# Blank products ahead of the first loads, word conversions behind the masks, and mixing steps in another order in an attention and mixer kernel

## The chip, the cores and the metric

The kernel runs on one core of one Trainium2 chip. Times are device microseconds (us) of one execution. The kernel before the change took 691.07 us, the median of three runs (690.26 to 691.5). The profiled execution spans 688.8 us from its first to its last instruction; that span is what the profile's views divide up.

A core has five engines that run at the same time and wait for one another by semaphores: TensorE (PE in the profile; PEld is its loading of weights), VectorE (DVE), ScalarE (ACT), GpSimd (POOL) and SyncE (SP). Each takes the instructions of its own queue in the order in which the program has them. In this kernel SyncE, and ScalarE at the very start, also issue the transfers from and to the chip's main memory.

## The reference, cut to what matters

A linear attention with decay, in blocks, is followed by a low-rank mixing over the sequence and a two-layer channel network with a residual:

```python
# q, k, v: (4, 8, 768, 64) float32; lam: (8,)
for b in range(nb):                                   # blocks of the sequence
    intra = einsum('bhic,bhjc->bhij', qb, kb) * Dmask     # Dmask = lam ** (i - j), lower triangle
    intra = einsum('bhij,bhjd->bhid', intra, vb)
    inter = einsum('bhid,bhde->bhie', qb * lam_pow, kv_state)
    out[:, :, sl] = intra + inter
    kv_state = lam_block * kv_state + einsum('bhsd,bhse->bhde', kb * rev_pow, vb)

x  = out as (4, 768, 512)
h  = x.transpose(0, 2, 1) @ U @ V                     # U: (768, 32), V: (32, 768)
u  = x + h.transpose(0, 2, 1)
ch = maximum(u @ w_ch1, 0) @ w_ch2                    # (512, 2048) and (2048, 512)
result = u + ch
```

U, V, w_ch1 and w_ch2 are float64 in memory. The kernel reads them as pairs of 32-bit words and puts together float32 values from them ("words" below).

## The kernel before

The attention part works on 24 tiles of 128 positions, six for each of the four batch rows, all eight heads at once. For a tile s: `prep` transposes q and k on TensorE and copies them out on ScalarE (tiles "qt", "kt"); `scores` multiplies them ("pss"); `masked` multiplies by the decay mask on VectorE ("sm"); `intra` multiplies by v ("px") and `state` updates the running state ("pkv", "kv"); `inter` adds the part of the state, with q scaled on GpSimd ("qs").

After the last tile of a row, `low` multiplies the row by U ("pp"), `low_sum` adds up the parts ("pr") and splits the result in a high and a low half ("vp"); `mix` multiplies by V and adds to the tile ("pu"); `turn` transposes the mixed tile for the channel network ("put"). `aside` does one portion of the conversion of words.

The order in which the pieces stand in every queue:

```python
    pieces = [("prep", 0), ("scale", 0), ("scores", 0), ("inter", 0), ("masked", 0)]
    for s in range(NS):
        b, c = divmod(s, NT)
        done = s - NT - 1
        more = s + 1 < NS
        step = [("prep", s + 1), ("scale", s + 1)] * more
        step += [("mix", done)] * (done >= 0)
        step += [("low", b - 1)] * (c == 0 and b > 0)
        step += [("intra", s), ("state", s)]
        step += [("turned", done - 1)] * (done > 0)
        step += [("scores", s + 1)] * more
        step += [("aside", s)]
        step += [("inter", s + 1), ("masked", s + 1), ("fade", s + 1)] * more
        step += [("low_sum", b - 1)] * (c == 0 and b > 0)
        step += [("turn", done)] * (done >= 0 and done // TG < FG)
        pieces += step
    pieces += [("mix", NS - NT - 1)]
```

One step of the word conversion, with two passes on VectorE and two on ScalarE; the portions that follow it are VectorE's alone:

```python
        def one():
            hi = st["w"][:, :, 1]
            ...
            nc.vector.tensor_scalar(sc, hi, 20, 0x7FF, ALU.logical_shift_right, ALU.bitwise_and)
            nc.vector.tensor_scalar(m, hi, 0xFFFFF, 0x100000, ALU.bitwise_and, ALU.bitwise_or)
            ...
            nc.scalar.activation(out=sc_f, in_=sc, func=AF.Relu, bias=low_end, scale=-1.0)
            nc.scalar.activation(
                out=sc, in_=sc_f, func=AF.Relu, bias=high_end, scale=-float(1 << 23)
            )
```

V's last portions split the values in a high part (copied on ScalarE) and a low part (subtracted on VectorE), each for several groups of rows of "vp". The tiles in which each portion stands:

```python
        (u_side, (0, 2, 2, 2, 2)),
        (v_steps(), (1, 2, 3, 3, 4, 4, 4, 5, 6, 6)),
```

The start. lam becomes a row on all partitions by a product ("pl", "lamb"); `constants` and `powers` make the mask and the powers from it on VectorE with twelve scans:

```python
    nc.scalar.dma_start(out=lam_row[:, 0:H], in_=lam.unsqueeze(0))
    nc.vector.memset(lam_row[:, H:], 1.0)
    for name, engine in (
        ("q", nc.sync), ("k", nc.scalar), ("q", nc.sync), ("k", nc.scalar), ("v", nc.sync)
    ):
        load_next(name, engine)
    for name in "kvqkv":
        load_next(name)
    make_identity(nc, ident)
    make_gather()
    pl = one_bank([P, H], "pl", "pq")
    nc.tensor.matmul(out=pl, lhsT=lam_row[:, H:], rhs=lam_row[:, 0:H], start=True, stop=True)
    nc.vector.tensor_copy(out=lamb, in_=pl)
    constants()
    scale_k(0)
    powers()
```

The channel network begins while the last row is still being mixed. Each unit is 16 products "pz" and 8 products "pd", evacuated to "r" by ScalarE and VectorE; the pieces of the last row are put between them (unit, product, piece, tile):

```python
    rest = [
        (0, 4, "enter", None),
        (0, 4, "turn", c0 - 2), (0, 9, "low", b), (0, 14, "low_sum", b),
        (0, 18, "turn", c0 - 1), (0, 22, "mix", c0),
    ]
    at = [(1, 5), (1, 13), (1, 21), (2, 5), (2, 13), (2, 21)]
    for n, (unit, i) in enumerate(at):
        if n + 1 < NT:
            rest.append((unit, i - 3, "mix", c0 + n + 1))
        rest.append((unit, i, "turn", c0 + n))
    ...
    side = list(zip((0, 1, 2, 2, 3, 3, 4, 4), w1_steps(2)))
```

The rest of the kernel, the two layers of the network, is the same before and after.

Of the kernel before, what the change touches and what calls it, by code (L numbers as in the profile page):

```python
# [8 lines left out]
FP32 = mybir.dt.float32  # L9
# [5 lines left out]
P = 128  # L15
# [3 lines left out]
def kernel(  # L19
# [59 lines left out]
    def set_ends(t):  # L79
        nc.vector.memset(t[:, 0:1], 1151.0)  # L80
        nc.vector.memset(t[:, 1:2], 255.0 * (1 << 23))
        ends.append(t)
# [184 lines left out]
    set_ends(vp[:, S + C : S + C + 2].bitcast(FP32))  # L267
# [55 lines left out]

    def prep(s):
        qt, kt = (att.tile([P, HP, P], FP32, tag=n, bufs=2, name=n) for n in ("qt", "kt"))
        n = HP // parts(s)
        for a0 in range(0, HP, n):
            for name, dst, tag in (("q", qt, "pt" if a0 else "pq"), ("k", kt, "pu" if a0 else "pk")):
                pt = one_bank([P, n, P], "p" + name, tag)
                for a in range(a0, a0 + n):  # L330
                    nc.tensor.transpose(  # L331
                        out=pt[:, a - a0, :], in_=raw[s, name][:, 2 * a : 2 * a + 2, :],
                        identity=ident,
                    )
                nc.scalar.copy(dst[:, a0 : a0 + n, :], pt)  # L335
        st[s].update(qt=qt, kt=kt)
        for name in "qk":
            load_next(name)
# [95 lines left out]
    def low(b):  # L434

        pp = one_bank([P, C], "pp", "pq") if b < B - 1 else bank([P, C], "pp", "b2")
        for c in range(G):
            nc.tensor.matmul(
                out=pp[c * R : (c + 1) * R, :], lhsT=u_w[:, c, :], rhs=xs[b * NT + c],
                start=True, stop=False,  # L440
            )

        n = C // 2
        assert 2 * (NT - G) == G
        for i in range(G):
            c, cols = G + i // 2, slice(i % 2 * n, (i % 2 + 1) * n)
            nc.tensor.matmul(
                out=pp[i * R : (i + 1) * R, cols], lhsT=u_w[:, c, :],
                rhs=xs[b * NT + c][:, cols], start=False, stop=True,
            )  # L450
        pts[b] = tmp("pt")
        nc.scalar.copy(pts[b], pp)

    def low_sum(b):
        pr = one_bank([P, C], "pr", "pu") if b < B - 1 else bank([P, C], "pr", "b2")
# [11 lines left out]
    def mix(s):  # L467
        b, c = divmod(s, NT)
        pu = one_bank([P, C], "pu", "pu") if s < NS - NT else bank([P, C], "pu", "b2")
# [48 lines left out]
    for s in range(NS):  # L518
# [3 lines left out]
        step = [("prep", s + 1), ("scale", s + 1)] * more  # L522
        step += [("mix", done)] * (done >= 0)
        step += [("low", b - 1)] * (c == 0 and b > 0)
# [3 lines left out]
        step += [("aside", s)]  # L528
        step += [("inter", s + 1), ("masked", s + 1), ("fade", s + 1)] * more
        step += [("low_sum", b - 1)] * (c == 0 and b > 0)  # L530
        step += [("turn", done)] * (done >= 0 and done // TG < FG)
        pieces += step
    pieces += [("mix", NS - NT - 1)]
# [55 lines left out]
    for steps, at in (  # L589
        (u_side, (0, 2, 2, 2, 2)),  # L590
        (v_steps(), (1, 2, 3, 3, 4, 4, 4, 5, 6, 6)),
# [13 lines left out]
    lam_row = consts.tile([1, H + P], FP32, name="lam_row")  # L605
    nc.scalar.dma_start(out=lam_row[:, 0:H], in_=lam.unsqueeze(0))
    nc.vector.memset(lam_row[:, H:], 1.0)
    for name, engine in (
        ("q", nc.sync), ("k", nc.scalar), ("q", nc.sync), ("k", nc.scalar), ("v", nc.sync)
    ):  # L610
        load_next(name, engine)
    for name in "kvqkv":
        load_next(name)
    make_identity(nc, ident)
    make_gather()
    pl = one_bank([P, H], "pl", "pq")
# [95 lines left out]
    def run_units(units, side, every=lambda i: None):  # L712
# [10 lines left out]
        (0, 4, "turn", c0 - 2), (0, 9, "low", b), (0, 14, "low_sum", b),  # L723
# [3 lines left out]
    at = [(1, 5), (1, 13), (1, 21), (2, 5), (2, 13), (2, 21)]  # L727
# [6 lines left out]
    side = list(zip((0, 1, 2, 2, 3, 3, 4, 4), w1_steps(2)))  # L734
# [162 lines left out]
```

## Time and profile before

| What | Before |
|---|---|
| median of three runs | 691.07 us |
| profiled span | 688.8 us |
| TensorE busy, share of the span | 98% |
| VectorE busy | 73% |
| ScalarE busy | 42% |
| GpSimd busy | 16% |
| transfers | 131.24 MB, 191 GB/s on the mean |

In the views that follow, the first number of a line of a timeline is the start in us from the beginning of the span, the second the duration; then come the engine, the line of the program, the operation, what it writes and reads, and how many instructions are merged. A bracket gives the time for which the engine was idle before it and what ended that. In the chain of work that ended last, each line is a start, a duration and what the end of the program waited for at that time. In a table by windows, each engine has its busy time and its count of instructions.

Attention and the last mixing fill the first 162 us of the span. The channel network fills the rest.

### The profile page before, as it was taken

To read this page: it belongs to the slowest core of one execution; us is meant where nothing else is said; L and a number is where in the kernel's file an instruction comes from. 1 tells how busy PE (TensorE), PEld (TensorE's weight loads), DVE (VectorE), ACT (ScalarE), POOL (GpSimd) and SP (SyncE) were. 2 spreads that over 40 slices of the span, in tenths; PEclk is the share of its full clock that TensorE was granted. 3 is DMA by queue.
4 is the path that set the end of the run, shared out by engine and by line. 5 is a ranking of instruction groups with operands and counts; after the bars stand their busy time and mean duration, and the time that the engine had idled before them with its cause. 6 is when DMAs were issued, how large, how long until landed. Compare 5 with 4: busy or idle time off the path is not lost.

```text
span 688.8 us, 12548 instructions
## 1 busy us (share of the span) xinstructions
PE 673.1 (98%) x4802; PEld 544.4 (79%) x4802; DVE 502.4 (73%) x857; ACT 290.5 (42%) x543; POOL 112.0 (16%) x90
## 2 busy tenths in 40 slices
PE   8889999999999999999999999999999999999997
PEld 6768787877888888888888888888888888888885
DVE  6468898877999777777789354787586686775864
ACT  4557676655566444444456231232232322322320
POOL 4326565532000000000000000030030120300300
PEclk9999999999999999999999999999999999999999
DMA  9968876235577655555566999955254363453431
GB/s 215 215 163 209 213 199 168 88 119 194 202 256 259 214 199 199 207 206 207 204 234 240 319 310 354 339 172 187 101 178 132 91 205 101 143 166 97 161 90 62
DMA packets 131629, 131.24 MB, mean 191 GB/s; under 512 B 81330, under 2 KB 89522, under 8 KB 131570
## 3 DMA queue, kind: packets, MB, share of 16 engines
q1 hardware_dynamic: 129472, 129.92, 59.1%
q8 instruction: 38, 0.62, 0.4%
q10 hardware_dynamic: 2098, 0.52, 0.3%
q14 instruction: 21, 0.17, 0.1%
HBM read 80.09 MB, written 50.33 MB: 189 GB/s over the span
## 4 chain that ended last, share of the span: by engine, by line
PE 93%; DVE 4%; DMA 1%; ACT 1%; issue 1%; POOL 0%; ACTq 0%; SPq 0%; DVEq 0%
PE pz L667 26%; PE pz L800 13%; PE pz L798 13%; PE pd L802 13%; PE pd L677 13%; PE px L424 3%; PE pss L371 3%; PE pkv L389 1%; PE px L412 1%; PE put L487 1%; PE pq L331 1%; PE pk L331 1%; DVE sm L380 1%; PE pu L470 1%; DMA words<-in_moe_V_dram 1%
## 5 line engine op out<-in xcount | busy, mean ns | idle before, releaser
L667 PE MATMUL pz<-u_hl,w 128*128 128x512 f32 x768 | 190.8, 398 | 0.8 <-ACT r L673 0.8
L667 PEld LDWEIGHTS pz<-u_hl,w 128*128 128x128 f32 x768 | 144.1, 188 | 37.0 <-ACT r L673 1.8
L800 PE MATMUL pz<-w_hl,m 128*128 128x512 f32 x384 | 151.6, 396 | 0.0
L798 PE MATMUL pz<-w_hl,m 128*128 128x512 f32 x384 | 151.6, 396 | 0.0
L802 PE MATMUL pd<-w_d,m 128*128 128x512 f32 x384 | 150.0, 396 | 0.0
L781 ACT ACTIVATE m<-mt 128x512 fp32r<-128x512 f32 x96 | 60.7, 632 | 195.3 <-PE pd L802 144.9
L782 DVE SCALAR_TENSOR_TENSOR m<-rm,m 128x512 fp32r<-128x512 f32 x96 | 71.5, 745 | 54.2 <-ACT m L781 54.1
L822 POOL TENSOR_TENSOR o<-o,u 128x512 f32<-128x512 f32 x20 | 29.9, 1524 | 450.7 <-DVE o L820 450.7
L682 DVE SCALAR_TENSOR_TENSOR r<-pd,r 128x512 f32<-128x512 f32 x96 | 61.8, 685 | 56.5 <-ACT r L673 44.2
L677 PE MATMUL pd<-u_d,w 128*128 128x512 f32 x384 | 98.8, 397 | 0.0
L798 PEld LDWEIGHTS pz<-w_hl,m 128*128 128x128 f32 x384 | 72.3, 188 | 17.6
L800 PEld LDWEIGHTS pz<-w_hl,m 128*128 128x128 f32 x384 | 72.3, 188 | 17.6
L802 PEld LDWEIGHTS pd<-w_d,m 128*128 128x128 f32 x384 | 72.3, 188 | 17.6
L677 PEld LDWEIGHTS pd<-u_d,w 128*128 128x128 f32 x384 | 72.1, 188 | 17.3
L673 ACT ACTIVATE r<-pz 128x512 f32<-128x512 f32 x96 | 51.9, 593 | 74.0 <-PE pz L667 73.9
L783 DVE SCALAR_TENSOR_TENSOR m<-m 128x512 fp32r<-128x512 f32 x96 | 69.1, 720 | 0.9
L780 DVE TENSOR_SCALAR mt<-rm 128x512 uint32<-128x512 uint32 x96 | 46.1, 481 | 24.6 <-DMA rm<-r_d 24.4
L380 DVE TENSOR_TENSOR sm<-pss,mask 128x512 f32<-128x512 f32 x48 | 30.7, 679 | 4.3 <-PE pss L371 4.3
L424 PEld LDWEIGHTS px<-vraw,sm 128*64 128x64 f32 x768 | 25.6, 142 | 10.3 <-DVE sm L380 5.3
L424 PE MATMUL px<-vraw,sm 128*64 128x64 f32 x768 | 29.5, 230 | 3.6 <-DVE sm L380 3.6
L355 POOL TENSOR_TENSOR qs<-qt,powq 128x512 f32<-128x512 f32 x20 | 25.6, 1278 | 40.7 <-ACT qt L335 37.4
L192 ACT CAST w<-wt 128x512 fp32r<-128x512 f32 x32 | 19.9, 622 | 29.0 <-DVE wt L189 20.7
(84 smaller groups left out, 706.4 us busy)
## 6 DMA issues: line engine op xcount, KB each, us to landing
r_d<-r SPq DMA_DIRECT2D x96, 256.0 KB, 2.2
rm<-r_d SPq DMA_DIRECT2D x96, 256.0 KB, 2.7
words<-in_moe_w_ch_dram SPq DMA_DIRECT2D x30, 512.0 KB, 4.1
w_d<-w SPq DMA_DIRECT2D x16, 768.0 KB, 3.3
w_hl<-w_d SPq DMA_DIRECT2D x16, 512.0 KB, 6.7
vraw<-in_v_dram SPq DMA_DIRECT2D x24, 256.0 KB, 3.8
u_d<-x_nat SPq DMA_DIRECT2D x24, 256.0 KB, 3.4
u<-u_d SPq DMA_DIRECT2D x24, 256.0 KB, 4.1
```

Source lines behind the costliest of these rows:

```text
L424: nc.tensor.matmul(out=px[half[t], x, a, :], lhsT=sm[:, x, a, half[t]], rhs=vr[:, 2 * a + x, :], start=(first and a == 0), stop=(a == HP - 1),
L667: nc.tensor.matmul(out=acc[g][0], lhsT=w[:, n, ct, :], rhs=uhl[g][:, n, ct, :], start=(ct == 0 and n == 0), stop=(ct == CT - 1 and n == 1),)
L673: nc.scalar.mul(rs[g], acc[g][0], 1.0 + E)
L677: nc.tensor.matmul(out=acc[g][1], lhsT=w[:, 2, ct, :], rhs=ud[g][:, ct, :], start=(ct == 0), stop=(ct == CT - 1),)
L682: nc.vector.scalar_tensor_tensor(rs[g], acc[g][1], 4096.0, rs[g], ALU.mult, ALU.add)
L780: nc.vector.tensor_scalar(t.bitcast(U32), r.bitcast(U32), HI, None, ALU.bitwise_and)
L781: nc.scalar.activation(out=m[:, 0], in_=t, func=AF.Relu)
L782: nc.vector.scalar_tensor_tensor(m[:, 1], r, 0.0, hi, ALU.max, ALU.subtract)
L783: nc.vector.scalar_tensor_tensor(m[:, 2], hi, E, low, ALU.mult, ALU.subtract)
L798: nc.tensor.matmul(out=pz, lhsT=m[:, 0, cols], rhs=hl[:, 0], start=first, stop=False)
L800: nc.tensor.matmul(out=pz, lhsT=m[:, 1, cols], rhs=hl[:, 1], start=False, stop=end)
L802: nc.tensor.matmul(out=pd, lhsT=m[:, 2, cols], rhs=dd, start=first, stop=end)
```

## The change

It has four parts.

1. Blank products: a tile of zeros is multiplied by itself, four times before lam's product and once before each of the first four groups of transposes. They compute nothing that is used; they are there to have TensorE at work while the first loads are under way. The first loads are issued in another order: q and k of tile 0 first, then lam, and all later loads from SyncE.
2. The word conversion of U and V stands behind the masks of the next tile instead of ahead of them, and some portions stand one tile later, so that a mask does not wait for words on their way.
3. At the boundary of two rows, `low` comes first in the step and `low_sum` before `intra`, so that copies and splits lie beside other products. They take other banks of the accumulator memory.
4. The mix of tile 17 moves from the end of the attention part into the first unit of the channel network, and the mixes and turns of the last row spread over three more units instead of two. Portions of the third weight tile's words move to later units.

```diff
+    def keep_busy(n, tag="pss"):
+        out = (one_bank([P, C], "idle", tag) if tag == "pq" else two_banks("idle", tag)[:, 0])[:, 0:P]
+        for i in range(n):
+            nc.tensor.matmul(out=out, lhsT=blank, rhs=blank, start=True, stop=True)
 ...
+                if s == 0:
+                    keep_busy(1)
 ...
-        pp = one_bank([P, C], "pp", "pq") if b < B - 1 else bank([P, C], "pp", "b2")
+        pp = one_bank([P, C], "pp", "pu") if b < B - 1 else bank([P, C], "pp", "b2")
 ...
-        pr = one_bank([P, C], "pr", "pu") if b < B - 1 else bank([P, C], "pr", "b2")
+        pr = one_bank([P, C], "pr", "pt") if b < B - 1 else bank([P, C], "pr", "b2")
 ...
-        step = [("prep", s + 1), ("scale", s + 1)] * more
-        step += [("mix", done)] * (done >= 0)
-        step += [("low", b - 1)] * (c == 0 and b > 0)
+        step = [("low", b - 1)] * (c == 0 and b > 0)
+        step += [("prep", s + 1), ("scale", s + 1)] * more
+        step += [("mix", done)] * (0 <= done < NS - NT - 1)
+        step += [("low_sum", b - 1)] * (c == 0 and b > 0)
         step += [("intra", s), ("state", s)]
         step += [("turned", done - 1)] * (done > 0)
         step += [("scores", s + 1)] * more
-        step += [("aside", s)]
+        step += [("aside", s)] * (done >= 0)
         step += [("inter", s + 1), ("masked", s + 1), ("fade", s + 1)] * more
-        step += [("low_sum", b - 1)] * (c == 0 and b > 0)
+        step += [("aside", s)] * (done < 0)
         step += [("turn", done)] * (done >= 0 and done // TG < FG)
         pieces += step
-    pieces += [("mix", NS - NT - 1)]
 ...
-        (u_side, (0, 2, 2, 2, 2)),
-        (v_steps(), (1, 2, 3, 3, 4, 4, 4, 5, 6, 6)),
+        (u_side, (0, 2, 2, 3, 3)),
+        (v_steps(), (1, 2, 4, 4, 5, 5, 5, 6, 6, 6)),
 ...
+    blank = x_pool.tile([P, C], FP32, tag="x", name="blank")[:, 0:P]
+    nc.vector.memset(blank, 0.0)
+    nc.vector.memset(lam_row[:, H:], 1.0)
+    set_ends(vp[:, S + C : S + C + 2].bitcast(FP32))
+    load_next("q", nc.sync)
+    load_next("k", nc.scalar)
     nc.scalar.dma_start(out=lam_row[:, 0:H], in_=lam.unsqueeze(0))
-    nc.vector.memset(lam_row[:, H:], 1.0)
-    for name, engine in (
-        ("q", nc.sync), ("k", nc.scalar), ("q", nc.sync), ("k", nc.scalar), ("v", nc.sync)
-    ):
-        load_next(name, engine)
-    for name in "kvqkv":
+    for name in "qkvkvqkv":
         load_next(name)
     make_identity(nc, ident)
     make_gather()
-    pl = one_bank([P, H], "pl", "pq")
+    keep_busy(4, "pq")
+    pl = one_bank([P, H], "pl", "pk")
 ...
-        (0, 4, "turn", c0 - 2), (0, 9, "low", b), (0, 14, "low_sum", b),
+        (0, 4, "turn", c0 - 2), (0, 6, "mix", c0 - 1), (0, 9, "low", b), (0, 14, "low_sum", b),
 ...
-    at = [(1, 5), (1, 13), (1, 21), (2, 5), (2, 13), (2, 21)]
+    at = [(1, 5), (1, 16), (2, 3), (2, 14), (3, 3), (3, 10)]
 ...
-    side = list(zip((0, 1, 2, 2, 3, 3, 4, 4), w1_steps(2)))
+    side = list(zip((0, 3, 3, 3, 4, 4, 4, 4), w1_steps(2)))
```

More of the change, by code (lines that the diff above doesn't have):

```diff
@@ L266 @@
     v_hl, p_hl = vp[:, 0:S], vp[:, S : S + C]
-    set_ends(vp[:, S + C : S + C + 2].bitcast(FP32))
     ident = keep.tile([P, P], FP32, name="ident")
@@ L468, in mix @@
         b, c = divmod(s, NT)
-        pu = one_bank([P, C], "pu", "pu") if s < NS - NT else bank([P, C], "pu", "b2")
+        pu = one_bank([P, C], "pu", "pu") if s < NS - NT - 1 else bank([P, C], "pu", "b2")
         nc.tensor.matmul(
```

## The prediction

> **What bounds the kernel now.** I read the page first: the span, the busy time of each engine and the shares of the chain that ended last.
>
> ```profile
> span 688.8 us, 12548 instructions
> ...
> PE 673.1 (98%) x4802; PEld 544.4 (79%) x4802; DVE 502.4 (73%) x857; ACT 290.5 (42%) x543; POOL 112.0 (16%) x90
> ...
> PE 93%; DVE 4%; DMA 1%; ACT 1%; issue 1%; POOL 0%; ACTq 0%; SPq 0%; DVEq 0%
> ```
>
> TensorE is busy for 673.1 of 688.8 us. From 162 us on its only hole is the end of the last product, which the change does not touch, so all that can be gained lies in the other 15.7 us of idle time and in the time in which TensorE ran at a lower speed. I then read the timeline of the first 12 us (start, duration, engine, line, idle time before and what ended it).
>
> ```profile
> 0.73 0.53 ACTq L606 DMA_DIRECT2D lam_row<-in_lam_dram  x1
> ...
> 2.05 0.56 PE L617 MATMUL pl<-lam_row 1*128 1x8 f32 x2 [2.05 <-DMA lam_row<-in_lam_dram]
> ...
> 2.85 2.63 DVE L288 TENSOR_TENSOR_SCAN mask<-lamb,ident 128x128 f32<-128x128 f32 x8
> ...
> 5.46 0.69 PE L331 MATMUL pk<-ident,kraw 128*128 128x128 f32 x2
> ...
> 6.08 2.08 PE L371 MATMUL pss<-qt,kt 64*128 64x128 f32 x16
> ...
> 6.89 2.19 DVE L301 TENSOR_TENSOR_SCAN powq<-small 128x128 f32<-128x128 f32 x4
> ...
> 9.00 1.26 DVE L380 TENSOR_TENSOR sm<-pss,mask 128x512 f32<-128x512 f32 x2
> 9.00 1.06 PE L331 MATMUL pk<-ident,kraw 128*128 128x128 f32 x4
> ...
> 9.99 1.48 PE L424 MATMUL px<-vraw,sm 128*64 128x64 f32 x32
> ```
>
> Two things are to be seen. The eight score products took 2.08 us here and take 1.16 us in every later tile: TensorE starts at about half speed, and still has it in the transposes at 9.00 (1.06 us, later 0.60), no longer in the state products at 11.30 (0.63, as later). And two chains reach the first "px" together: the loads of k (last half used at 5.46, then scores, then the next transposes) and the chain from lam, which lands at 2.05 and goes through the mask scans (2.63), the power scans (2.19) and "sm" (1.26), ending at 10.26. Neither has slack: "px" starts at 9.99.
>
> Then the chain that ended last, in order of time, for the attention part:
>
> ```profile
> 24.06 4.58 DMA words<-in_moe_V_dram
> ...
> 29.38 0.55 DVE m L158
> 29.93 1.21 DVE sm L380 x2
> ...
> 31.18 1.76 PE px L424 x28
> ...
> 49.26 0.47 PE pu L470
> ```
>
> Tile 3 and 4 of the first batch row wait on words of U and V, which stand on VectorE's queue ahead of "sm"; "px" of tile 4, which would have followed the transposes at 29.1, starts at 30.59 and goes on only at 31.18. The end shows the first mixing product waiting for the low half of p (1.31 us of idle time in the timeline). Two windows of 3.41 us at the place where the granted clock steps down (busy time of PE, PEld, DVE, ACT, POOL, then the granted clock and DMA) show the second price of that wait:
>
> ```profile
> 27.69:31.10 3.41, 1.74 (x40) 1.29 (x30) 2.34 (x5) 1.96 (x6) 0.00 (x0) 1.00 1.07 248
> 31.10:34.51 3.41, 3.33 (x50) 3.21 (x52) 0.62 (x3) 1.76 (x4) 2.63 (x3) 0.50 0.78 183
> ```
>
> TensorE was busy in only 1.74 of 3.41 us, and the following 3.41 us ran at a granted clock of 0.50. Last, the timeline of TensorE alone after 75 us; the brackets are all its waits that the change aims at:
>
> ```profile
> 113.73 0.47 PE L470 MATMUL pu<-vp 128*128 128x512 f32 x1 [0.35 <-DVE vp L463]
> ...
> 135.22 0.50 PE L470 MATMUL pu<-vp 128*128 128x512 f32 x1 [0.87 <-DVE x_nat L473]
> ...
> 156.70 0.63 PE L487 MATMUL put<-ident,x_nat 128*128 128x128 f32 x4 [0.25 <-DVE x_nat L473]
> ...
> 161.11 1.23 PE L667 MATMUL pz<-u_hl,w 128*128 128x512 f32 x3 [0.77 <-ACT r L673]
> ```
>
> [...]
>
> **The change part by part.**
>
> *Start.* Four blank products stand before lam's product, four more before the transposes of tile 0. A 512-column pass of "pr" follows its neighbour after 0.47 us, so 128 columns are 0.118 us, a blank product with two passes 0.24 us at full speed and about 0.47 at half: an estimate from that row. They start at about 1.1 us (after one more memset) and keep TensorE busy to 1.1 + 4 x 0.47 = 3.0. But lam's load moves from the first to the third place on ScalarE's queue, behind both halves of k. Issues there take 0.42 to 0.53 us, so it is issued at 0.73 + 0.53 + 0.43 + gaps = 1.75 instead of 0.73: one us later at the least. If it also stands in the rings behind k's 256 KB, it lands with them: q and k of tile 0 are 512 KB, first packets came 1.1 us after the issue (1.85), at some 220 GB/s they are in at 4.2, and 0.35 us passes to the product: lam at about 4.5 instead of 2.05, 2.4 us later. Everything on the lam chain keeps its length (2.05 to 10.26, 8.2 us), so "sm" ends near 12.7 instead of 10.26. TensorE itself: lam's product to 5.1, four pairs of a blank (0.47) and two transposes (0.55) to 9.2, scores to 10.2 at full or 11.2 at half speed, next transposes 1 to 2 us: 11.3 to 13. So the first "px" is ready about 2.4 us later, whatever the clock is. With the lesser delay of lam it is 0.9. The full clock comes too late to matter. I take +2.3 us.
>
> *U's and V's words behind the masks.* At full speed a tile takes 4.29 us (18.96 to 23.25), the first tile after the boundary about 5.6. From "px" of tile 2 at 18.96, with no wait at all, "px" of tile 3 would be at 23.25, of tile 4 at 27.54, of tile 5 at 31.83, of tile 6 at 36.53 (no state product, 1.5 us of "pp"), of tile 7 at 42.16. It was at 49.73: 7.6 us lost. In the new order I walk the queues again. VectorE does sm, then the words, so "px" waits no more; but ScalarE has two passes over the words (0.46 each for U, 0.62 for V) that stand ahead of the copies of the next q and k (pitch 0.47, 1.05 together).
> - U: sm(3) ends 22.93, first word step 0.3, ScalarE's two to 24.2, copies to 25.25; scores of tile 4 were due at 24.82: 0.5 lost.
> - V: sm(5) ends 1.32 after its scores, words 0.35, ScalarE's two to 2.96, copies to 4.0; the next scores are due at 2.73: 1.3 lost.
> - Boundary: V's last steps follow sm(6) (to 1.3) and end at 2.55, ScalarE's two casts of 0.5 each to 3.6, "pt" to 4.2. Its sum product is due at 2.5, as low and low_sum now come before the first "px" of the new row: 1.7 lost.
> - V's low rows (four of 0.55) come after sm(7) and end at 3.6 after its scores, while the first mix is due at 1.65: 1.95 lost.
> That is 5.4 instead of 7.6: 2.2 gained. Two of the new waits are as long as the one that halved the clock; one more window at half costs what it cost before, 1.76 + 1.07 + 1.52 against 1.15 + 0.64 + 1.16, 1.4 us; I put half of that in: gain 1.5.
>
> *Boundaries 2 and 3.* low starts one us earlier, with the transposes between it and low_sum, so the copy "pt" (0.58) is covered, and the low half of p (two of 0.7) is finished long before the next mix. That takes away 0.35 twice, and about 0.1 twice of the wait for "pp": gain 0.9.
>
> *Last mixing.* mix of tile 17 leaves its place ahead of the first big product (wait 0.87) for a place inside it, and the turns spread over a fourth unit, which relieves VectorE, ScalarE and GpSimd where the 0.25 and the 0.77 arose. Turn 23 is issued with 14 products of 0.234 us to go, 3.3 us before its data is first needed; its low part takes 0.05 + 0.7 + 0.6 + 0.6 + 1.3, about 3.3: just in time. Gain 1.9, at the most.
>
> Sum: +2.3 - 1.5 - 0.9 - 1.9 = -2.0, 691.1 to **689.1 us**.
>
> **Rivals.** (1) lam is hardly late. For it: 32 bytes in one packet. Then the start costs 0.9 or, if the clock comes early enough to speed tile 0, nothing: 687.7 to 686.8. (2) The first row gains more: if GpSimd's passes no longer collide, the word steps are shorter (V's third took 1.33 us beside two GpSimd passes, against 0.36 for U's) and one of the four new waits falls away: about 687.5. Against it: they are ScalarE's, not VectorE's. (3) The new waits halve the clock twice and lam's chain lets it idle once more: 691 to 692. (4) VectorE becomes the bound after the front: it was busy 19.51 of 20 us from 180 to 200, and three word steps of the third weight tile and a turn and a half are pushed towards it. Late evacuations would cost one to two us; against it, no idle time of TensorE there in the trace and two sets of banks.
>
> **Range and chances.** Start 0.5 to 3, words gain 0 to 3.5, boundaries and last mixing gain 2 to 2.8: 684.8 to 692.1 with all ends at once, which is unlikely. I take 686.2 to 691.6. Two per cent is 13.8 us, nearly all the idle time there is; so within 2% has 0.98, the others 0.01 each.
>
> **What would show it.** In the timeline of the changed kernel: lam's product starting at 4 us or later, with TensorE idle between the blanks and it, and "sm" of tile 0 ending after 12 (step 1); score products at about 1.1 us only from tile 1 on; no wait of "px" for "sm" in tiles 3 to 5, but waits of "pss" for the copies of k, of "pr" for "pt", and of the first "pu" for "vp" (step 2); no such wait at the second and third boundary (step 3); no gap before the first big product (step 4). I am wrong if "px" of tile 0 starts near 10 us or earlier, or if a window at half clock stands in the first 60 us more than once.

## The result, and the profile after

The changed kernel took 690.25 us (median of four runs, 689.71 to 690.47) against 690.88 us (four runs, 690.26 to 691.5) for the kernel before, measured beside it. The ratio is 0.999 with a 95% interval of 0.9972 to 1.0007: no difference that these runs could show. The prediction was 689.1, and its range of 686.2 to 691.6 holds the result. The range also holds the time of the kernel before, though, and the gain of 2.0 us that the prediction's sum came to lies just outside the interval, which runs from 1.9 us less to 0.5 us more. The parts of the sum say more than the total.

The profile's page of the changed kernel says the same, the span, the busy times and the shares of the chain that ended last:

```profile
span 688.6 us, 12580 instructions
...
PE 674.0 (98%) x4818; PEld 546.5 (79%) x4818; DVE 498.8 (72%) x858; ACT 291.2 (42%) x543; POOL 112.2 (16%) x90
...
PE 94%; DVE 3%; ACT 2%; issue 1%; DMA 0%; ACTq 0%; DVEq 0%
```

The span is 0.2 us shorter, TensorE is busy for 0.9 us more, with the blank products counted in, and the chain is TensorE's as before. So gains and losses of the four parts cancelled. To see which gained, I read the start of four landmark instructions of TensorE in both timelines; the difference grows or shrinks between two landmarks by what lies between them.

| Landmark | Before | After | Difference | Share of the stretch |
|---|---|---|---|---|
| first state product "pkv" of tile 0 | 11.30 | 13.60 | +2.30 | start: +2.30 |
| "px" of tile 7 | 49.66 | 52.71 | +3.05 | words, first boundary: +0.75 |
| "px" of tile 23 | 133.20 | 135.18 | +1.98 | boundaries 2 and 3: -1.07 |
| "pd" of the fourth unit | 165.22 | 165.19 | -0.03 | last mixing: -2.01 |

The four lines in TensorE's timeline before:

```profile
11.30 0.63 PE L389 MATMUL pkv<-vraw,ks 128*64 128x64 f32 x16
...
49.66 1.15 PE L424 MATMUL px<-vraw,sm 128*64 128x64 f32 x32
...
133.20 1.15 PE L424 MATMUL px<-vraw,sm 128*64 128x64 f32 x32
...
165.22 2.04 PE L677 MATMUL pd<-u_d,w 128*128 128x512 f32 x8
```

and after:

```profile
13.60 0.64 PE L396 MATMUL pkv<-vraw,ks 128*64 128x64 f32 x16
...
52.71 1.15 PE L431 MATMUL px<-vraw,sm 128*64 128x64 f32 x32
...
135.18 1.15 PE L431 MATMUL px<-vraw,sm 128*64 128x64 f32 x32
...
165.19 2.04 PE L686 MATMUL pd<-u_d,w 128*128 128x512 f32 x8
```

The start, from the timeline of the changed kernel (start, duration, engine, line, operation, in brackets the idle time before it and what ended it):

```profile
0.74 1.09 ACTq L255 DMA_DIRECT2D kraw<-in_k_dram  x2
...
1.05 2.08 PE L327 MATMUL idle<-blank 128*128 128x128 f32 x8 [1.05 <-DVE blank L614]
...
1.85 0.61 ACTq L619 DMA_DIRECT2D lam_row<-in_lam_dram  x1
...
4.65 0.56 PE L626 MATMUL pl<-lam_row 1*128 1x8 f32 x2 [1.52 <-DMA lam_row<-in_lam_dram]
...
5.45 2.63 DVE L287 TENSOR_TENSOR_SCAN mask<-lamb,ident 128x128 f32<-128x128 f32 x8
...
8.58 2.93 DVE L300 TENSOR_TENSOR_SCAN powq<-small 128x128 f32<-128x128 f32 x4
...
8.85 1.58 PE L378 MATMUL pss<-qt,kt 64*128 64x128 f32 x16
...
11.43 1.26 DVE L387 TENSOR_TENSOR sm<-pss,mask 128x512 f32<-128x512 f32 x2
...
12.14 0.34 PE L431 MATMUL px<-vraw,sm 128*64 128x64 f32 x4 [0.67 <-DVE sm L387]
```

lam's load is issued at 1.85 and no longer at 0.73, and its product runs at 4.65 and no longer at 2.05, after the blanks and 1.52 us of idle time. Mask scans, power scans and "sm" follow one another from there, and "px" starts at 12.14. That the score products took 1.58 us here instead of 2.08 changes nothing: "px" waits for "sm".

The waits that took the place of the old ones, from TensorE's timeline of the changed kernel:

```profile
27.40 0.69 PE L396 MATMUL pkv<-vraw,ks 128*64 128x64 f32 x16 [0.76 <-ACT kt L342]
...
37.36 1.16 PE L378 MATMUL pss<-qt,kt 64*128 64x128 f32 x16 [1.16 <-ACT kt L342]
...
42.88 1.13 PE L463 MATMUL pr<-pt,gather 128*128 128x512 f32 x2 [1.91 <-ACT pt L459]
43.94 1.97 PE L431 MATMUL px<-vraw,sm 128*64 128x64 f32 x32
...
52.30 0.47 PE L477 MATMUL pu<-vp 128*128 128x512 f32 x1 [2.52 <-DVE vp L582]
```

and from its later part:

```profile
160.23 1.22 PE L676 MATMUL pz<-u_hl,w 128*128 128x512 f32 x3 [0.20 <-ACT r L682]
```

The old waits of "px" for "sm" in tiles 3 to 5 are gone. In their place stand 0.76, 1.16, 1.91 and 2.52 us, the first three for a copy that stands behind words in ScalarE's queue, the last for V's own low rows, which VectorE splits off last. From 60 us on only 0.20 us of waiting is left. The line at 43.94 shows the further price: 1.97 us for 32 products that take 1.15 elsewhere. The table by windows of the same kernel (busy time of PE, PEld, DVE, ACT, POOL, then granted clock and transfers) gives the cause:

```profile
40.49:43.91 3.42, 1.51 (x7) 0.54 (x5) 0.76 (x2) 2.45 (x5) 0.52 (x1) 1.00 0.82 196
43.91:47.32 3.41, 3.41 (x55) 3.27 (x56) 1.81 (x3) 1.25 (x3) 1.15 (x2) 0.50 0.02 4
50.73:54.15 3.42, 1.84 (x49) 1.63 (x49) 2.67 (x3) 0.24 (x1) 1.01 (x1) 1.00 0.65 148
```

TensorE was busy for 1.51 of 3.42 us, and the next 3.41 us ran at a granted clock of 0.50. The third line is a window of 1.84 us, with no half clock after it.

### The profile page after: what moved, and what is told of

It is laid out like the page before. It is cut to its first block, busy times and chain, and to the rows that moved or that the text cites. A ratio compares the mean times of both kernels' runs of the same rounds, so it can differ in the third digit from the quotient of the medians.

```text
span 688.6 us, 12580 instructions
## 1 busy us (share of the span) xinstructions
PE 674.0 (98%) x4818; PEld 546.5 (79%) x4818; DVE 498.8 (72%) x858; ACT 291.2 (42%) x543; POOL 112.2 (16%) x90
## 4 chain that ended last, share of the span: by engine, by line
PE 94%; DVE 3%; ACT 2%; issue 1%; DMA 0%; ACTq 0%; DVEq 0%
PE pz L676 26%; PE pz L809 13%; PE pz L807 13%; PE pd L686 13%; PE pd L811 13%; PE px L431 3%; PE pss L378 3%; PE put L494 2%; PE pkv L396 1%; PE px L419 1%; PE pq L338 1%; PE pk L338 1%; PE pu L477 1%; DVE sm L387 1%; PE pr L463 1%
## 5 line engine op out<-in xcount | busy, mean ns | idle before, releaser
L378 PE MATMUL pss<-qt,kt 64*128 64x128 f32 x384 | 28.6, 289 | 1.2 <-ACT kt L342 1.2
```

The lines of the kernel that those rows point to most:

```text
L378: nc.tensor.matmul(out=pss[:, x, a, :], lhsT=kt[half[x], a, :], rhs=qt[half[x], a, :], start=True, stop=True,)
```

## The experiments

All edits are made to the changed kernel where nothing else is said; "the start of before" is the old order of the first loads without blanks. Every ratio is to the kernel before, run beside it on the same chip. The changed kernel was timed only in the comparison above, where the kernel before took 690.88; beside the runs here that kernel took 691.18 to 691.32. So where a median is set against that of the changed kernel, or runs on different chips are set against each other, some 0.4 us more can be the chip's.

| Run | What is different | Median (runs) | Ratio, 95% interval |
|---|---|---|---|
| 1 | lam's load first | 689.0 (10) | 0.9968, 0.9955 to 0.9981 |
| 2 | no blanks | 690.31 (20) | 0.9986, 0.9978 to 0.9994 |
| 3 | start of before | 688.79 (6) | 0.9954, 0.9936 to 0.9972 |
| 4 | start and words of before | 686.67 (4) | 0.9932, 0.9917 to 0.9946 |
| 5 | last mixing alone | 688.58 (10) | 0.996, 0.995 to 0.9971 |
| 6 | blanks in the new waits | 689.11 (6) | 0.9968, 0.9956 to 0.9981 |
| 7 | words behind the copies | 685.79 (4) | 0.9921, 0.9907 to 0.9936 |
| 8 | words behind the copies and early, start of before | **681.32** (4) | 0.9855, 0.9839 to 0.9872 |
| 9 | as 8, all words earlier still | 681.95 (4) | 0.9865, 0.985 to 0.988 |
| 10 | as 8, lam first, powers behind the mask | 683.52 (4) | 0.9889, 0.9869 to 0.9908 |

### 1. lam's load first

```diff
+    nc.scalar.dma_start(out=lam_row[:, 0:H], in_=lam.unsqueeze(0))
     load_next("q", nc.sync)
     load_next("k", nc.scalar)
-    nc.scalar.dma_start(out=lam_row[:, 0:H], in_=lam.unsqueeze(0))
```

> The changed kernel with one line moved: lam's load is again the first on ScalarE's queue, ahead of both halves of k. My theory: the start is bound by the chain lam, mask scans, power scans, sm, so it follows lam's product. That now waits only for the four blank products (to about 3.1 us) instead of lam (4.65), so the first px comes about 1.5 us earlier (12.73 to about 11.2) and everything after it too: about 688.7 us against 690.25, and 1.1 us of the start still lost against the kernel before. Rival: the loads of q and k and the clock bind the start; then the first px moves by under 0.3 us, and the time stays at 690.2.

The timeline of this kernel's start:

```profile
3.06 0.59 PE L626 MATMUL pl<-lam_row 1*128 1x8 f32 x2
...
9.87 1.26 DVE L387 TENSOR_TENSOR sm<-pss,mask 128x512 f32<-128x512 f32 x2
...
10.58 0.34 PE L431 MATMUL px<-vraw,sm 128*64 128x64 f32 x4 [1.02 <-DVE sm L387]
```

One line has moved, and the product of lam runs at 3.06, right behind the four blanks; "sm" starts 1.56 us earlier than in the changed kernel and "px" too. The state product of tile 0, the first landmark, comes at 12.05. So lam's place makes 1.55 of the 2.30 us. The other 0.75 us stands here although lam is on time: its product runs 1.01 us later than before (2.05), as it now waits for the blanks (run 10, with two in place of four, has it at 2.20). The median is 1.25 us below that of the changed kernel. The waits of 1.16, 1.91 and 2.51 us in the first row are unchanged, a pause of 0.86 us stands where the 0.76 was, and this profile has two windows at half clock, not one.

The ten runs spread from 687.4 to 691.35, and their mean granted clocks, which are on record, go along with that. One window at half clock lowers the mean by 0.0025 (an estimate: half of 3.41 us in 689; the profiles of both kernels, with one such window each in the first row, have 0.998, and that of run 4, with none there, 0.999). The fastest of the ten has 1.000, the five from 688.22 to 689.04 have 0.997 or 0.998, the three from 689.72 to 690.1 have 0.994 or 0.995, and the slowest has 0.992. That fits none, one, two and three such windows.

### 2. No blanks

```diff
-                if s == 0:
-                    keep_busy(1)
...
-    keep_busy(4, "pq")
```

> The changed kernel without the eight blank products; lam's load stays third. My theory: the blanks neither help nor hurt, as lam's chain binds: lam's product again near 4.6 us, first px at 12.7 within 0.3 us, time within 0.5 us of the changed kernel's. Rival A (the blanks bring the full clock early and that pays): scores of tile 0 slower by up to 0.9 us and the first px later by as much. Rival B (the blanks delay the transposes and that costs): first px earlier by about a microsecond.

lam stays third in its queue, and its product starts at 4.86 with all 4.86 us before it idle for "DMA lam_row"; the scores of tile 0 take 2.08 us again, and "px" starts at 12.35 instead of 12.14. The median is that of the changed kernel within 0.1 us. The blanks do raise the clock earlier: in the four profiles with eight of them these scores take 1.25 to 1.58 us, in all others 2.08. That buys nothing, because "px" waits for the chain from lam. The twenty runs fall into groups by their granted clock once more: three with 1.000 took 688.85 to 688.93, nine with 0.996 to 0.998 took 689.65 to 690.56, seven with 0.994 took 690.97 to 691.26, and one with 0.991 took 692.9. So a window at half clock costs 1.0 to 1.2 us here, the third perhaps more.

### 3. The start of before

The order of the first loads, and with it the place of lam, goes back; words, boundaries and last mixing stay changed.

```diff
-    load_next("q", nc.sync)
-    load_next("k", nc.scalar)
     nc.scalar.dma_start(out=lam_row[:, 0:H], in_=lam.unsqueeze(0))
-    for name in "qkvkvqkv":
+    for name, engine in (
+        ("q", nc.sync), ("k", nc.scalar), ("q", nc.sync), ("k", nc.scalar), ("v", nc.sync)
+    ):
+        load_next(name, engine)
+    for name in "kvqkv":
         load_next(name)
...
-    keep_busy(4, "pq")
```

> The changed kernel with the start of the kernel before (no blanks, lam first, the second k on ScalarE's queue). My theory: 2.3 us under the changed kernel, 688.0 us, with the first px near 10.0 and all the waits of the first row as in the changed kernel (0.76, 1.16, 1.91, 2.52). Together with the run that has the later parts alone (686.7) it gives the price of the words' new order: 1.3 us. Rival: the delay of the start hid loads of words or tiles; then new waits for loads come up in the first 30 us and the time is above 689.

The first "pu" comes at 49.92 instead of 52.30, 2.38 us earlier: the +2.30 of the start, read a second way. The median fell by less, 1.46 us against that of the changed kernel. The row's waits are the same four (0.76, 1.17, 1.91, 2.52), but the profiled run has two windows at half clock. The granted clocks show what those cost: the two executions with 1.000 took 686.36 and 686.41 us, the four with 0.994 took 688.77 to 689.38. So the start was worth its term, and in four executions of six the clock took part of it away. Run 2 has no blanks either and differs from this run in the first loads, but for a memset and a bank; with the clock at 1.000 in both, it took 688.89 (the middle of three) against 686.39, so the order of the loads costs 2.5 us.

### 4. Start and words of before

Only boundaries and last mixing are changed here. Besides the start of run 3:

```diff
-        step += [("aside", s)] * (done >= 0)
+        step += [("aside", s)]
         step += [("inter", s + 1), ("masked", s + 1), ("fade", s + 1)] * more
-        step += [("aside", s)] * (done < 0)
...
-        (u_side, (0, 2, 2, 3, 3)),
-        (v_steps(), (1, 2, 4, 4, 5, 5, 5, 6, 6, 6)),
+        (u_side, (0, 2, 2, 2, 2)),
+        (v_steps(), (1, 2, 3, 3, 4, 4, 4, 5, 6, 6)),
```

> The kernel before with only the later parts of the change: low and low_sum in their new places and banks, and the last mixing over three units; start and words as before. My theory: these two parts gained what the first two lost. Boundaries two and three 1.0 us, last mixing 2.0 us: about 688 us, 3 us under the kernel before (ratio 0.9957). At the first boundary the sum product may wait for its copy for up to 1.5 us, which would leave 1.5. Rival: their gain is an effect of the delay ahead of them (VectorE with more time to catch up), then about 690.5.

Against run 3 the median is 2.1 us lower, and only the order of the words differs. But the two executions of run 3 with a full clock took 686.36 and 686.41 us, no more than the 686.67 here. So the old order is the better one by the clock that it keeps; that it is better at full clock too is not shown. TensorE's timeline of this run, the old waits for "sm":

```profile
25.33 0.34 PE L429 MATMUL px<-vraw,sm 128*64 128x64 f32 x4 [1.90 <-DVE sm L385]
...
31.64 0.34 PE L429 MATMUL px<-vraw,sm 128*64 128x64 f32 x4 [1.48 <-DVE sm L385]
...
38.00 0.34 PE L429 MATMUL px<-vraw,sm 128*64 128x64 f32 x4 [1.19 <-DVE sm L385]
```

With the second parts of these waits (0.26 each) that is 5.35 us, hardly less than the 6.35 of the new order. There is no half clock here: the first wait, 1.90 + 0.26, lies across two windows with 2.47 and 2.2 us of busy time.

The expectation of about 688 was 1.3 us too high, and the profile has other reasons for that. The half clock of the kernel before is gone (some 1.5 us, by the products of that window), and so are its waits of 0.29 and 1.31 us at the first boundary, while the waits for "sm" are longer, 5.35 us against 3.59. No wait at all is left at the first boundary up to the first "pu": part 3 of the change had made room there, and part 2 put V's last portions into just that place (the 1.91 and 2.52 of the changed kernel).

### 5. The last mixing alone

The kernel before, with part 4 only:

```diff
-        step += [("mix", done)] * (done >= 0)
+        step += [("mix", done)] * (0 <= done < NS - NT - 1)
...
-    pieces += [("mix", NS - NT - 1)]
...
-        (0, 4, "turn", c0 - 2), (0, 9, "low", b), (0, 14, "low_sum", b),
+        (0, 4, "turn", c0 - 2), (0, 6, "mix", c0 - 1), (0, 9, "low", b), (0, 14, "low_sum", b),
...
-    at = [(1, 5), (1, 13), (1, 21), (2, 5), (2, 13), (2, 21)]
+    at = [(1, 5), (1, 16), (2, 3), (2, 14), (3, 3), (3, 10)]
...
-    side = list(zip((0, 1, 2, 2, 3, 3, 4, 4), w1_steps(2)))
+    side = list(zip((0, 3, 3, 3, 4, 4, 4, 4), w1_steps(2)))
```

> The kernel before with the last part alone (mix of tile 17 inside the first unit, turns over three more units, the third weight tile's steps later). My theory: the waits of 0.87, 0.25 and 0.77 us before 161 us go, 0.2 comes: 1.7 us under the kernel before, 689.5, ratio 0.9975. The boundaries are then the rest of the gain of the run with the later parts alone. Rival: the gain is taken back behind it, where VectorE has less room: same time as before.

The waits of 0.87, 0.25 and 0.77 us at the end are gone, and 0.20 came: 1.69 in all. The median is 2.6 us lower than the 691.18 of the kernel before beside it, and the interval (2.0 to 3.5 us) just takes in the 2.01 of the table of landmarks. The first boundary still has its old 0.29 and 1.31.

### 6. Blanks in the new waits

Seven blank products stand before the sum product of the first row, nine before its first mix. They compute nothing that is used; they only keep TensorE at work where it waited.

```diff
+    def fill(n, tag):
+        out = one_bank([P, C], "idle", tag)[:, 0:P]
+        for i in range(n):
+            nc.tensor.matmul(out=out, lhsT=blank, rhs=blank, start=True, stop=True)
...
+        if b == 0:
+            fill(7, "pt")
...
+        if s == 0:
+            fill(9, "pu")
```

> The changed kernel with blank products also where TensorE waits in the first row: seven (about 1.7 us at full clock) ahead of the sum product, whose wait is 1.91, and nine (about 2.2) ahead of the first mix, whose wait is 2.52. They need nothing and can lie wholly in the waits. My theory: the half clock after those waits is the answer to an idle TensorE and not to anything else; with the waits filled no window at 0.50 is left in the first 60 us and the time falls by one to two windows' price, 1.4 to 2 us, to about 688.5. Rival: the clock has another cause, or the blanks delay the products behind them: the same time or up to 0.5 us more.

TensorE's timeline of this kernel:

```profile
40.78 1.73 PE L332 MATMUL idle<-blank 128*128 128x128 f32 x14
42.85 1.13 PE L470 MATMUL pr<-pt,gather 128*128 128x512 f32 x2 [0.35 <-ACT pt L464]
43.91 1.15 PE L436 MATMUL px<-vraw,sm 128*64 128x64 f32 x32
...
48.10 2.17 PE L332 MATMUL idle<-blank 128*128 128x128 f32 x18
50.80 0.47 PE L486 MATMUL pu<-vp 128*128 128x512 f32 x1 [0.52 <-DVE vp L591]
```

The blanks take 1.73 and 2.17 us of the two waits, and the waits' ends stay: the sum product begins at 42.85 (42.88 in the changed kernel). But "px" at 43.91 takes 1.15 us instead of 1.97, no window from 9.22 to 63.83 us is at half clock, and the first "pu" begins at 50.80, 1.50 us earlier than in the changed kernel. So the half clock was the answer to TensorE's idle time in the window before (busy for 1.51 of 3.42 us in the changed kernel, for 3.06 of 3.41 here), and it cost the 1.5 us that the prediction had put at 1.4 and then halved. The median fell by 1.14 us. All six executions have a mean clock of 0.999 or 1.000; the four of the changed kernel have 0.996 to 0.998. The waits here end when another engine's chain does, as at the start; what pays is the full clock behind them, which at the start nothing could use.

### 7. Words behind the copies

The two ScalarE passes of a word step are what "kt" stands behind. From the timeline of ScalarE in the changed kernel:

```profile
35.09 0.61 ACT L149 ACTIVATE sc<-sc,vp 64x384 f32<-64x384 uint32 x1 [2.56 <-DVE sc L145]
35.74 0.61 ACT L150 ACTIVATE sc<-sc,vp 64x384 uint32<-64x384 f32 x1
36.26 0.56 ACT L342 COPY qt<-pq 128x512 f32<-128x512 f32 x1
36.73 0.58 ACT L342 COPY kt<-pk 128x512 f32<-128x512 f32 x1
```

Two passes of 0.61 us from 35.09, then the copies "qt" and "kt", the second of which ends at 37.31; "pss" starts at 37.36. The edit takes the words of the previous tile right behind the copies of the next one, and V's portions a tile earlier:

```diff
         step += [("prep", s + 1), ("scale", s + 1)] * more
+        step += [("aside", s - 1)] * (0 < s <= NT + 1)
...
-        step += [("aside", s)] * (done < 0)
...
-        (v_steps(), (1, 2, 4, 4, 5, 5, 5, 6, 6, 6)),
+        (v_steps(), (0, 1, 3, 4, 4, 4, 4, 5, 5, 5)),
```

> The changed kernel with the portions of U's and V's words put after the transposes and copies of the next tile (so that ScalarE's two passes come after the copies of q and k, not ahead of them), V's loads one tile earlier and V's low rows before the sum product's split. My theory: the four waits of the first row (0.76, 1.16, 1.91, 2.52 us) and the window at half clock (1.5 us) are the order of ScalarE's and VectorE's queues and go away: first mix at about 45 us instead of 52.3, time about 683 us. Rival: the work itself is too much for these engines there, or the words land too late; then other waits of the same sum come up (masks again behind words, or V's load), and under 2 us is gained.

The four waits and the half clock are gone, and the median is 4.5 us below that of the changed kernel. It stays 2.8 us above the expected 683, since new waits came. One of them, from the timeline of all engines:

```profile
30.31 1.27 POOL L362 TENSOR_TENSOR qs<-qt,powq 128x512 f32<-128x512 f32 x1 [3.02 <-DMA qraw<-in_q_dram]
30.37 1.43 DVE L145 TENSOR_SCALAR sc<-words 64x384 uint32<-64x384 uint32 x1
...
31.55 2.30 POOL L351 TENSOR_TENSOR ks<-kraw,small 128x512 f32<-128x512 f32 x2
31.73 1.21 DVE L146 TENSOR_SCALAR m<-words 64x384 uint32<-64x384 uint32 x1
...
33.66 0.69 PE L419 MATMUL px<-kv,qs 64*64 64x64 f32 x32 [1.03 <-ACT x_nat L436]
```

V's two word passes took 1.43 and 1.21 us beside GpSimd's products, and 0.34 and 0.35 in the changed kernel, where GpSimd had nothing to do. The ScalarE pass, the copy "x_nat" behind it and the waiting "px" (1.03 us) all shift. Further waits were 0.69 us (for "kv", on VectorE behind V's low rows, 3.22 us, and the split of p), 1.38 + 0.26 (for "sm", behind words of the channel weights that came late from memory) and 0.84.

### 8. Words early and behind the copies, with the start of before

Besides the start of run 3, U's words are loaded right after the first loads, and all portions of U and V stand so that they are done at tile 6:

```diff
+        step += [("aside", s - 1)] * (0 < s <= NT + 3)
...
-        step += [("aside", s)] * (done >= 0)
+        step += [("aside", s)] * (s >= NT + 3)
...
-        step += [("aside", s)] * (done < 0)
...
-        (u_side, (0, 2, 2, 3, 3)),
-        (v_steps(), (1, 2, 4, 4, 5, 5, 5, 6, 6, 6)),
-        (w1_steps(0, True), (3, 4, 5, 6, 7, 8, 9, 10, 12, 13, 14)),
+        (u_side, (-1, 1, 1, 2, 2)),
+        (v_steps(), (0, 0, 2, 3, 3, 4, 4, 4, 5, 5)),
+        (w1_steps(0, True), (3, 4, 5, 6, 8, 9, 10, 11, 12, 13, 14)),
...
+    aside(-1)
```

> The later parts of the change, the start of the kernel before, and the words once more in another order: behind the copies of the next tile, but a tile earlier than in the last such run (U is loaded with the first tiles, V in the first step), so that no portion is longer than the gap on VectorE, and the third operand's first conversion step one tile later and behind the copies too. My theory (every wait of the first row is an order of queues, and the start costs 2.3 us): 685.8 of that run less 2.3 for the start less the four waits left there (1.03, 0.69, 1.64, 0.84): about 680 us, ratio 0.984. Rival: VectorE beside GpSimd is too slow for any order there; then new waits of the same sum appear, about 683.5.

This version beats both kernels: 681.32 us, 1.45% under the kernel before (interval 1.28 to 1.61%). Two lines of its page, and three of TensorE's timeline from 12 to 62 us:

```profile
span 679.4 us, 12547 instructions
...
PE 669.7 (99%) x4802; PEld 542.4 (80%) x4802; DVE 497.8 (73%) x857; ACT 291.3 (43%) x543; POOL 111.4 (16%) x90
```

```profile
27.14 0.69 PE L417 MATMUL px<-kv,qs 64*64 64x64 f32 x32 [1.03 <-ACT x_nat L434]
...
42.68 0.48 PE L475 MATMUL pu<-vp 128*128 128x512 f32 x1
...
56.80 0.69 PE L417 MATMUL px<-kv,qs 64*64 64x64 f32 x32 [1.10 <-ACT x_nat L434]
```

Two waits of about a microsecond are left, and no half clock. "px" of tile 7 follows "pu" at 43.09; the prediction's walk without any wait had 42.16 for it, so the 1.03 us is about all that the first row still loses. Both remaining waits are for "x_nat", behind words on ScalarE. Run 4 has the same start and the same later parts, so the new place of the words is worth 5.3 us against their old one.

### 9. All words earlier still

```diff
-        (u_side, (-1, 1, 1, 2, 2)),
-        (v_steps(), (0, 0, 2, 3, 3, 4, 4, 4, 5, 5)),
+        (u_side, (-1, 0, 0, 1, 1)),
+        (v_steps(), (-1, -1, 2, 2, 3, 3, 3, 4, 4, 5)),
```

against run 8, with the words behind the copies only up to tile 7.

> As the run with the early words and the start of before, with U and V loaded right behind the first tiles' loads, every portion one more tile earlier, and the third operand's first step back ahead of the mask of tile 8. My theory: the two waits left there (1.03 for x_nat behind V's passes, 1.10 for x_nat behind the passes over the first weight tile) go, 0.5 may stay of the second: 681.3 less 1.0 to 1.6, about 680.0 us. Rival: the earlier loads push the tiles' loads back and transposes wait: 681 or more.

A miss: no gain, 0.6 us slower than run 8 by the medians, on another chip and with overlapping intervals. The 1.03 at 27.14 and the 1.10 at 56.80 are gone, but 0.85 came at 18.27 (for "kv"), 1.08 at 32.30 (for "x_nat") and 0.15 + 0.26 at 54.08 (for "sm"). Moving the word passes further only moved the wait.

### 10. lam first, powers behind the mask, on top of run 8

The chain from lam to "px" carries four power scans that "sm" of tile 0 does not need. Here they come after it, with loads in the new order but lam first, and four blanks.

```diff
-    pieces = [("prep", 0), ("scale", 0), ("scores", 0), ("inter", 0), ("masked", 0)]
+    pieces = [("prep", 0), ("scale", 0), ("scores", 0), ("inter", 0), ("masked", 0), ("powers", 0)]
...
-    powers()
```

> As the run with the early words and the start of before, but with lam first, two blank products ahead of lam's product and one ahead of each transposition of k, and the four power scans behind the first masks instead of ahead of them. My theory: with the power scans out of the chain lam to sm, the loads and TensorE bind: first px at 9.0 to 9.8 us instead of 10.0; the power scans then end near 12 and the first state product (12.96 before) may wait up to 0.5. Net 0 to 0.8 us under that run. Rival: the blanks delay the transposes at half clock by 0.5 us each and give it back: 0 to 1 us above it.

A miss again. "px" of tile 0 starts at 10.07 (run 8: 10.14): with the power scans out of the way, VectorE waits 2.84 us for the scores before "sm", and these for the loads of q and k. And V's words came later, in the timeline of all engines:

```profile
21.82 1.23 SPq L131 DMA_DIRECT2D words<-in_moe_V_dram  x2
...
27.17 0.35 DVE L145 TENSOR_SCALAR sc<-words 64x384 uint32<-64x384 uint32 x1 [3.39 <-DMA words<-in_moe_V_dram]
...
29.39 0.69 PE L419 MATMUL px<-kv,qs 64*64 64x64 f32 x32 [3.31 <-DVE sm L387]
```

V's words were asked for at 21.82 (run 8: 19.68), and VectorE waited 3.39 us for them; "sm" stood behind, and "px" waited 3.31 us. A window at half clock followed. Loads, blanks and power scans changed together here, so this run alone doesn't say which of them made V's words late. Of the orders tried at the start, none did better than the old one.

## Why the prediction was right where it was, and wrong where it was

**The start, +2.3: measured +2.30.** Issue in third place, lam's product (4.5 foreseen, 4.65 measured), "sm" ending near 12.7 (12.69), and the clock coming too late to matter all went as written. The 4.5 rested on an assumption, that lam lands with k when it is issued behind it, and the kernel before has no load that shows this; in the changed kernel the 32 bytes moved at 3.91 us, while k's second half was on its way (3.3 to 4.3). Runs 2 and 3 show that the order of the loads is the cause, run 3 that the whole start is worth its 2.4 us. The blanks neither help nor hurt as long as lam comes late (run 2); with lam first, 0.75 us is left in run 1, where lam's product stands behind them.

**The words, -1.5: measured +0.75.** This is the term that was mis-sized, and its sign turned with it. The mechanism was as written, waits for copies behind ScalarE's word passes and for "vp", and the same number of them. The first was foreseen at "pss" and came one product earlier, at "pkv", for the same copy "kt": it writes to the bank that "pk" leaves free once "kt" is copied. The sizes: 0.5, 1.3, 1.7 and 1.95 foreseen, 0.76, 1.16, 1.91 and 2.52 measured, 0.9 us more together (6.35 against 5.45). Most of that is the last one: one of the four subtractions of V's low rows took 1.53 us beside GpSimd's "qs", the other three 0.55 each. The half clock was put in by half, 0.7 us; it came in full, 1.97 + 1.07 + 1.45 against 1.15 + 0.64 + 1.16, 1.5 us, and run 6 gave 1.50 back at the first mix. Together that is 1.7 of the 2.25 us by which the term was off. The rest, some 0.5, is spread over small stretches of the timelines and rounding, and I can't assign it. The prediction's own numbers had two waits as long as the one which had halved the clock, so one window in full was the better guess for the two together. No single wait is sure to cost: the one of 2.52 us was followed by full clock in the profile of the changed kernel and by half clock in those of runs 1, 2 and 3.

**What the term had left out** is that parts 2 and 3 use the same place. Run 4 shows that with V's words at their old places the first boundary is free of waits; part 2 filled it up. A sum of parts, each compared with the kernel before, could not see it.

**Boundaries 2 and 3, -0.9: measured -1.07. Last mixing, -1.9: measured -2.01.** Both as written: no wait stands at those boundaries, and none before the first big product. The 0.20 that came at 160.23 is the "just in time" of turn 23. Run 5 gives the last part alone.

**The range.** With all ends at once the lower end is 691.1 + 0.5 - 3.5 - 2.8 = 685.3 and not 684.8; the range that the prediction took does not rest on it. By the landmarks the sum missed the forecast by 2.0 us: 2.25 in the words, less the 0.28 by which the last two terms did better. By the medians it is 1.4, a gain of 0.6 against 2.0.

**The rivals.** That lam is hardly late fell with the 4.65. That the first row gains more fell with the table of landmarks, though runs 7 and 8 show that a gain of that kind was there for another order. That the clock halves twice did not happen in the profile of the changed kernel, and did in those of runs 1 and 3, which share its words and boundaries; the mean clocks of seven of run 2's twenty executions (0.994) fit two such windows as well. That VectorE becomes the bound after the front fell: no wait of TensorE there is longer than 0.20 us.

## What to carry to other kernels

When work is put aside behind the instruction that used to wait for it, walk every queue it uses: two ScalarE passes of 0.61 us ahead of the next copies cost as much as the passes ahead of the mask had. Put such work right behind the copies that TensorE waits for next, as early as its data allow; that was worth 5.3 us here (run 8 against run 4), and with the old start and the later parts of the change 1.45% against the kernel before. Before keeping a unit busy with blank work, ask what comes behind it: blanks gave nothing at the start, where a later chain set the time, and 1.1 us of the median in the first row, where they kept the clock up.

## What the runs showed of the hardware that I had not expected

- **Half clock behind windows with 1.74 us of work or less.** Once it was full, the granted clock changed on a grid of 3.41 us: in the kernel before it is full from 10.62 to 31.10 us, six times 3.41, and at 0.50 to 34.51; in the changed kernel it is full from 9.77 to 43.91, ten times 3.41, and at 0.50 to 47.32. A window with TensorE busy for 1.74 us (before) or less (1.51 in the changed kernel, 1.16 in run 5, 0.65 in run 10) was followed by one at 0.50. Windows with 1.76 us (run 7), 1.84 (the changed kernel) and 2.01 (run 2) were not. Run 7's, in the form of the table above:

```profile
50.11:53.52 3.41, 1.76 (x26) 1.32 (x26) 2.46 (x5) 1.96 (x5) 0.00 (x0) 1.00 0.85 224
53.52:56.93 3.41, 2.56 (x70) 2.24 (x68) 2.56 (x5) 3.41 (x10) 2.41 (x3) 1.00 0.30 70
```

  1.74 and 1.76 us are 0.51 and 0.52 of a window. An estimate from the two puts the bound in these profiles near 0.51, if the busy times are good to a hundredth; they are modelled ends, so this is rough. The busy time of weight loads divides these windows as well (1.29 and less against 1.32 and more), so which of the two counts stays open. A single wait of 1.91 us was enough in the changed kernel, where it lay within one window (1.51 us busy). The first wait of run 4, 1.90 + 0.26 us, was cut by the grid into windows with 2.47 and 2.20 us of work, and no half clock followed. The grid lies elsewhere in each profile (a window begins at 10.62 in the kernel before and at 11.04 in run 8, whose start is the same). That would explain why executions of one program differ in their mean clock; each window at half clock, counted from that mean, went with 1.0 to 1.3 us in runs 2 and 3. In the kernel before, the executions hardly differ by it: of the 29 executions beside runs 1, 2, 4 and 7, sixteen with a mean clock of 0.999 or 1.000 have a median of 691.23, ten with 0.997 or less one of 691.69. Its later waits in the first row may take up the loss; no run tests that.
- **VectorE beside GpSimd.** V's two word passes, which took 0.34 and 0.35 us in the changed kernel, where GpSimd had nothing to do, took 1.43 and 1.21 us in run 7, where it was at work. In the run 7 lines above, the pass that starts at 30.37, beside a GpSimd product ending at 31.58, ends at 31.80. What held it up, the traces don't show.
- **A small load in third place.** lam's load has 32 bytes. Issued at 0.73, its product ran at 2.05; issued at 1.85 behind k's two halves, at 4.65. The issue was 1.12 us later, the product 2.60: less than half of the delay is the issue's. In the record of packets the 32 bytes move at 1.63 and at 3.91 us, the latter while k's second half is on its way (3.3 to 4.3). This agrees with the prediction's assumption that lam lands with k. But q's packets are on their way as well, from 1.84 us on, and no run tells k's share of the delay from q's.
